# Attention products of whole units: two half-unit passes become one, in a new order of a step pair

## The chip, the cores and the metric

The kernel runs on one core of a Trainium2 chip, in one launch. The metric is the device time of that launch in microseconds (us); lower is better. It is given as the median of several runs. One further execution was recorded by the hardware profiler, and all rows quoted here come from such an execution. Names of engines in the rows: PE is the matmul engine (TensorE), PEld its weight loads, DVE VectorE, ACT ScalarE, POOL GpSimd, SP the engine that issues most of the DMAs.

## The reference

Four layers over an input of 2048 rows and 640 columns in float32, each added to its input after a layer norm: windowed attention, Fourier mixing, attention, Fourier mixing.

```python
def _A_ref(x, wqkv, wo):                  # H = 32 heads, Dh = 20, W = 8, dil = 2
    q, k, v = (x @ wqkv) split in three, (B, H, S, Dh)
    idx = pos[:, None] - (jnp.arange(W) * dil)[None, :]
    mask = idx >= 0
    kg, vg = k[:, :, idx], v[:, :, idx]   # (B, H, S, W, Dh), idx clipped at 0
    logits = jnp.einsum("bhsd,bhswd->bhsw", q, kg) * Dh ** -0.5
    attn = softmax(jnp.where(mask, logits, -1e9))
    o = jnp.einsum("bhsw,bhswd->bhsd", attn, vg)
    return o.transpose(0, 2, 1, 3).reshape(B, S, D) @ wo

def _B_ref(x, Ws_re, Ws_im, Wd_re, Wd_im):
    a, b = x @ Wd_re.T, x @ Wd_im.T
    return Ws_re @ a - Ws_im @ b

x = x + _A_ref(_layernorm(x), ...)
x = x + _B_ref(_layernorm(x), ...)
x = x + _A_ref(_layernorm(x), ...)
x = x + _B_ref(_layernorm(x), ...)
```

Each row attends to itself and the seven rows at distances 2, 4, ... 14 before it, so q·k and attn·v are eight products of 20 elements for each row and head.

## The kernel before

Every large product runs on PE in three passes over operands split in a rounded high part and a remainder (a "hi" copy on ACT, a "lo" subtraction on DVE or POOL). [...]

**Tiling of attention.** The 2048 rows are four chunks c of 512 (even rows, then odd rows); a partition holds four rows of a chunk. The 32 heads are eight groups e of four (80 columns). A unit u is one chunk and one group, u = 8c + e, 32 units in a layer. A unit's window tile holds 11 consecutive rows of k (or v) for each partition, and a strided view gives each of its four rows its eight. The units of the last chunk (24 to 31, `PAIRED`) are formed differently: two rows of a partition and two groups of heads, with one window tile for each group.

**What a unit does**, in two halves (jp) of two rows each until now. The product q·k (L423, DVE, 128 partitions by 2·8·80 = 1280 elements, q from PSUM, k from the window), then POOL adds elements 10 to 19 of each head to elements 0 to 9 (L425, 640 elements), then DVE sums the ten (L431) into the logits lg. After both halves the softmax runs once over the unit's 128 logits a partition: mask (L446, in chunks 0 and 2 only), max (L448), subtraction (L450), exp on ACT (L439), sum (L452), reciprocal (L454), weights pp (L456). Then again in halves the product of weights and v (L461, DVE, 1280 elements), and a tree of three adds over the eight window rows on POOL (L476 with 640 elements, L477 with 320, L478 with 160), the last of which writes the output tile (zo0 to zo3). Unit 31's second half has its tree on DVE.

**Buffers.** The products go through a ring of four tiles pr0 to pr3 of two rows each. The windows have a ring of five tiles (`NWIN`), loaded by SP (L409) in the order of use. q comes by a DMA (L393) to one tile qs, and ACT copies it to PSUM (L396, `q_copy`) before the unit's products. One PSUM tile, pq, holds q, the weights pp, the max, the sum and the mask side by side. Waits between engines are made for a whole tile.

**Order.** All engines run in program order, and the order in attention is written out by hand: a plan maps (step, phase) to functions, and a loop goes through steps −7 to 66 and, in each, through the names in `PHASES`. Two steps are one unit's pitch. Before, unit u has its half products at steps 2u and 2u+1 (phase qk), the reduces one step later (red1, red0), mask, max, subtraction and exp at 2u+2, sum, reciprocal and pp at 2u+3, the half av products and trees at 2u+3 (av1) and 2u+4 (av0), and its q copy at 2u−1.

**Around it in the same steps.** On PE: the qkv projections of later chunks (L354, from step −7 on), transposes of normed x and of the attention output (L319, L327), the output projection (L501), and from step 49 on the first matmuls of the next Fourier layer (L916, `z_mm`) in thirds, their number a step given by `ZTHIRDS`. On DVE in phase misc: the residual adds (L151), splits of the output weights (L555) and of Fourier matrices (L901), the lo part of the next layer's normed input (L866, on POOL or DVE). On ACT: evacuations of qkv (L361), hi and lo parts of transposes (L323, L342), row statistics. `TA` is the step of the transposes of the last chunk's rows j = 2, 3 (first three column blocks); the last two blocks and the rest of the output projection follow the loop. The Fourier layers share `T(...)`, the allocator of tiles by tag, and hold some of their weights in the tiles pr0 to pr3.

Of the kernel before, what the change touches and what calls it, by code (L numbers as in the profile page):

```python
# [20 lines left out]
D = 640  # L21
H = 32
DH = 20
# [25 lines left out]
)  # L49
TA = 65  # L50
NWARM = 18
# [20 lines left out]
def tile_layers(ctx: ExitStack, tc: tile.TileContext, x, wqkv, wo, cs, wre, wim, out):  # L72
# [161 lines left out]
    def layer_a(li, stats, handoff, prev):  # L234
# [6 lines left out]
        xnT = {}  # L241
        pcnt = [0]
        mt = {}
# [14 lines left out]

        def prod():
            pcnt[0] += 1  # L260
            return T([P, 2, W, FE], f"pr{pcnt[0] % 4}")

# [136 lines left out]
        def w_load(u, t, i=None):  # L399
            c = u // NE  # L400
            e, jp = half(u, i or 0)
            r0 = (c % 2) * 512
            if i is not None:
                r0 += 2 * jp
            n = SLOTS if i is None else SLOTS - 2
            b = kvb[e // 2][c // 2][e % 2, t, r0 : r0 + n, :]
            src = bass.AP(tensor=b.tensor, offset=b.offset, ap=[[NJ * FE, P], [1, n * FE]])
            w = wtile([P, SLOTS * FE])
            nc.sync.dma_start(w[:, : n * FE], src)  # L409
            if i is None:  # L410
                for x in range(2):
                    win[(u, x, t)] = (w, 2 * x * FE)
            else:
                win[(u, i, t)] = (w, 0)

        def wview(u, i, t, tail):
            w, off = win.pop((u, i, t))
            return bass.AP(tensor=w.tensor, offset=w.offset + off, ap=[w.ap[0], [FE, 2], [FE, W]] + tail)

        def qk_mul(u, jp):  # L420
            pr = prod()
            q = qs[u][:, 2 * jp : 2 * jp + 2].unsqueeze(2).to_broadcast([P, 2, W, FE])
            nc.vector.tensor_tensor(pr, q, wview(u, jp, 0, [[1, FE]]), op=ALU.mult)  # L423
            pv = pr.rearrange("p j w (h d) -> p (j w h) d", d=DH)
            nc.gpsimd.tensor_tensor(pv[:, :, 0:10], pv[:, :, 0:10], pv[:, :, 10:20], op=ALU.add)  # L425
            prq[(u, jp)] = pv

        def qk_red(u, jp):
            if jp == 0:
                lgs[u] = T([P, NJ, W, HE], "lg", bufs=2)  # L430
            nc.vector.tensor_reduce(  # L431
                lgs[u][:, 2 * jp : 2 * jp + 2].rearrange("p j w h -> p (j w h)"),
                prq.pop((u, jp))[:, :, 0:10],
                axis=AX.X,
                op=ALU.add,
            )
# [21 lines left out]

        def av_mul(u, jp):
            pr = prod()  # L460
            nc.vector.tensor_tensor(  # L461
                pr.rearrange("p j w (h d) -> p j w h d", d=DH),
                lgs[u][:, 2 * jp : 2 * jp + 2].unsqueeze(4).to_broadcast([P, 2, W, HE, DH]),
                wview(u, jp, 1, [[DH, HE], [1, DH]]),
                op=ALU.mult,
            )
            avq[(u, jp)] = pr

        def av_tree(u, i):
            c = u // NE  # L470
            e, jp = half(u, i)
            if e == 0:
                oo[(c, jp)] = T([P, 2, D], f"zo{(2 * c + jp) % 4}")
            pr = avq.pop((u, i))
            g = nc.vector if (u, i) == (NG - 1, 1) else nc.gpsimd
            g.tensor_tensor(pr[:, :, 0:4], pr[:, :, 0:4], pr[:, :, 4:8], op=ALU.add)  # L476
            g.tensor_tensor(pr[:, :, 0:2], pr[:, :, 0:2], pr[:, :, 2:4], op=ALU.add)  # L477
            g.tensor_tensor(oo[(c, jp)][:, :, e * FE : (e + 1) * FE], pr[:, :, 0], pr[:, :, 1], op=ALU.add)  # L478

# [123 lines left out]
        def prologue_first():  # L603
            wq_begin(0)
            for j, (k0, k1) in enumerate(((0, 3), (3, 5))):
                x_load(0, j, f"pr{j}")
                for k in range(k0, k1):
                    wq[(0, k)] = wq_load1(0, k)
            for j in range(2, NJ):
                x_load(0, j, f"pr{j}")  # L610
            for q in (1, 2, 3):
# [144 lines left out]
        for c, w, xtags in (  # L756
# [19 lines left out]
        for ph in ("peT0", "hi", "peL", "actL"):  # L776
            plan.pop((67, ph))
        at(66, "pe3w", wo_mm, c, 2, ("aux0", "aux1"), 0, 2, 0, 3)
        for i in range(2):
            at(65, "dmas", *((handoff.cw_load, 0) if first else (handoff.c_get,)), 14 + i)  # L780
        at(65, "dmar", r_load, c, 2, "xr")
        at(66, "dmar", r_load, c, 3, "xa")
        if prev is not None:
            for j2 in range(2):
                at(j2 - 3, "pe3", prev.ymm, NT - 1, j2, 0, KD)
                at(j2 - 2, "actl", prev.yout, NT - 1, j2, stats)
        last = 66
        thirds = [t for t, n in ZTHIRDS[ly].items() for _ in range(n)]
# [14 lines left out]
        else:  # L803
            at(63, "dmac", handoff.c_get, 13)

        PHASES = (
            "peT0 dma evac hi pe peL pe2 fin red0 dma2 qk sA sB av0 sD red1 sE sC exp evacA actL evacO actl sF av1 qc"
            " dmaw dmas misc dmac dmar pe3w pe3"
        ).split()
        with tc.manual_schedule(engines=ENGINES):  # L810
# [7 lines left out]
            pc_pe(67)  # L818
            pc_hi(67)
            pc_lo(67, True)  # L820
            wo_mm(c, 2, None, 0, 2, 3)
# [22 lines left out]
    class LayerB:  # L844
# [79 lines left out]
        def load_w(self):  # L924
            self.wr = T([P, 2, KD, D], "r2a", F32R)
            self.wi = []
            for k in range(KD):
# [3 lines left out]
                if k < 4:  # L931
                    wt = T([P, 2, D], f"pr{k}", F32R)
                    hl = (wt[:, 0], wt[:, 1])
# [383 lines left out]
```

## Time and profile before

| | |
|---|---|
| median of 3 runs | 1813.44 us (1812.18 to 1818.15) |
| the profiled execution, its own time | 1810.4 us |
| its span in the profile | 1808.5 us |
| mean granted PE clock | 0.992 |
| layer 0, attention | about 0 to 400 us of the span |
| layer 2, attention | about 940 to 1290 us |

A row of the view by line reads: line of the kernel, engine, operation, output tile <- input tiles with their shapes, count; then the total busy us and the mean ns of one; then the engine's idle time just before these instructions and what ended it. A row of the timeline has start, length, engine, line and operation. In the slices each digit is the busy share of a fortieth of the span (45 us) in tenths, and the chain is the work that ended last, followed back from the last instruction.

### The profile page before, as it was taken

The numbers are of one execution on the slowest core, as the hardware profiler recorded it, in microseconds if no ns is written. First come the engines' busy times: TensorE is split into PE (matmuls) and PEld (weight loads), VectorE is DVE, ScalarE is ACT, GpSimd is POOL, SyncE is SP. The second block draws the span as 40 slices with busy tenths as digits, with TensorE's granted clock in tenths as the row PEclk, the third lists the DMA queues.
The fourth block names the chain that finished last, engine by engine and source line by source line (L and its number), as shares of the span: only waits on it lengthen the run. The fifth ranks groups of instructions, "written<-read, shape, count | busy, mean of one in ns | idle before, by whom it ended". The sixth has DMA issues, their size and how long they took to land.

```text
span 1808.5 us, 26471 instructions
## 1 busy us (share of the span) xinstructions
PE 1746.1 (97%) x8798; PEld 1508.9 (83%) x8798; DVE 1380.1 (76%) x2129; ACT 818.9 (45%) x1708; POOL 640.6 (35%) x597
## 2 busy tenths in 40 slices
PE   9999997989999999999999999999899999999999
PEld 6879886777887887888888889877788888888888
DVE  5899899888768767767739988887777677676673
ACT  5544544544445445445533334444434443443441
POOL 3799898960000000000008987899400000000000
PEclk9999998999999999999999999999999999999999
DMA  6776667647789689677647856687687766876761
GB/s 233 224 263 208 208 203 247 218 164 280 273 267 332 223 270 336 221 258 229 215 132 226 278 181 199 200 296 261 218 295 257 259 226 225 265 231 223 259 210 52
DMA packets 273738, 423.59 MB, mean 234 GB/s; under 512 B 22688, under 2 KB 152736, under 8 KB 273344
## 3 DMA queue, kind: packets, MB, share of 16 engines
q1 hardware_dynamic: 270400, 419.92, 70.0%
q10 hardware_dynamic: 3200, 1.97, 0.4%
q8 instruction: 70, 1.15, 0.2%
q14 instruction: 68, 0.56, 0.1%
HBM read 336.66 MB, written 85.14 MB: 233 GB/s over the span
## 4 chain that ended last, share of the span: by engine, by line
PE 65%; DVE 12%; DMA 10%; POOL 6%; ACT 3%; issue 3%; SPq 1%; DVEq 0%; ACTq 0%; POOLq 0%
PE m L354 17%; PE aux L994 13%; PE t L1083 9%; PE m L1083 9%; PE xt L1083 4%; PE pq L1083 4%; PE aux L501 4%; DMA win<-cs_in 2%; DVE pr L423 2%; DVE pr L461 2%; PE m L916 2%; PE t L916 2%; POOL pr L476 2%; DMA c0b<-r 2%; DVE r L1077 1%
## 5 line engine op out<-in xcount | busy, mean ns | idle before, releaser
L354 PE MATMUL m<-r,s 128*128 128x480 f32 x1920 | 439.9, 384 | 5.7 <-ACT s L224 2.4
L354 PEld LDWEIGHTS m<-r,s 128*128 128x128 f32 x1920 | 357.5, 189 | 61.5 <-ACT s L224 3.8
L166 POOL TENSOR_TENSOR stats<-stats,mhalf 128x1 f32<-128x1 f32 (+1 forms) x40 | 30.4, 761 | 564.9 <-ACT stats L162 564.8
L1076 ACT CAST r<-win 128x512 fp32r<-128x512 f32 x244 | 149.4, 620 | 178.4 <-DVE win L1112 75.5
L994 PE MATMUL aux<-r2a,zo 128*128 128x320 f32 x768 | 226.5, 310 | 0.0
L476 POOL TENSOR_TENSOR pr<-pr 128x640 f32<-128x640 f32 x126 | 200.9, 1595 | 40.7 <-DVE pr L461 39.7
L423 DVE TENSOR_TENSOR pr<-pq,win 128x1280 f32<-128x1280 f32 x128 | 189.8, 1483 | 29.9 <-ACT pq L396 29.3
L994 PE MATMUL aux<-pr,zo 128*128 128x320 f32 x704 | 208.2, 308 | 0.0
L1077 DVE TENSOR_TENSOR r<-win,r 128x512 fp32r<-128x512 f32 x244 | 164.5, 686 | 46.8 <-ACT r L1076 40.7
L461 DVE TENSOR_TENSOR pr<-pq,win 128x1280 f32<-128x1280 f32 x128 | 190.8, 1491 | 4.5 <-DVE pq L456 0.2
L425 POOL TENSOR_TENSOR pr<-pr 128x640 f32<-128x640 f32 x128 | 183.4, 1433 | 18.7 <-DVE pr L423 15.6
L1083 PE MATMUL m<-r,r 128*128 128x512 f32 x600 | 154.7, 392 | 0.4 <-DVE r L1077 0.4
L994 PEld LDWEIGHTS aux<-r2a,zo 128*128 128x128 f32 x768 | 144.1, 188 | 2.0
L1083 PE MATMUL t<-r,r 128*128 128x512 f32 x498 | 135.4, 393 | 2.5 <-issue 2.5
L916 PE MATMUL m<-s,r 128*128 128x512 f32 x384 | 119.8, 399 | 15.3 <-DMA s<-c0b 6.7
L1083 PEld LDWEIGHTS m<-r,r 128*128 128x128 f32 x600 | 112.4, 188 | 25.8 <-DVE r L1077 0.7
L994 PEld LDWEIGHTS aux<-pr,zo 128*128 128x128 f32 x704 | 132.1, 188 | 2.0
L916 PE MATMUL t<-s,r 128*128 128x512 f32 x384 | 118.4, 395 | 2.3 <-DVE ot L976 1.5
L361 ACT COPY stg<-m 128x480 f32<-128x480 f32 x128 | 70.9, 556 | 104.6 <-PE m L354 94.0
L477 POOL TENSOR_TENSOR pr<-pr 128x320 f32<-128x320 f32 x126 | 114.4, 908 | 9.9
L431 DVE TENSOR_REDUCE lg<-pr 128x64 f32<-128x640 f32 x128 | 103.9, 811 | 17.7 <-POOL pr L425 17.4
L1083 PEld LDWEIGHTS t<-r,r 128*128 128x128 f32 x498 | 93.4, 188 | 24.6 <-issue 3.3
(269 smaller groups left out, 3246.3 us busy)
## 6 DMA issues: line engine op xcount, KB each, us to landing
win<-cs_in SPq DMA_DIRECT2D x358, 256.0 KB, 4.1
r<-xc SPq DMA_DIRECT2D x240, 256.0 KB, 4.3
win<-kvb SPq DMA_DIRECT2D x96, 440.0 KB, 4.8
xa<-cs_in SPq DMA_DIRECT2D x124, 256.0 KB, 4.2
win<-kvb SPq DMA_DIRECT2D x64, 360.0 KB, 5.3
xc<-stg SPq DMA_DIRECT2D x40, 512.0 KB, 3.1
kvb<-stg SPq DMA_DIRECT2D x60, 320.0 KB, 3.9
xr<-xs SPq DMA_DIRECT2D x40, 320.0 KB, 3.2
```

The source lines that it names most:

```text
L354: nc.tensor.matmul(mt[g][:, : 3 * F], st[:, a, k], wq[q][:, b, k], start=n == 0, stop=n == 14)
L423: nc.vector.tensor_tensor(pr, q, wview(u, jp, 0, [[1, FE]]), op=ALU.mult)
L425: nc.gpsimd.tensor_tensor(pv[:, :, 0:10], pv[:, :, 0:10], pv[:, :, 10:20], op=ALU.add)
L431: nc.vector.tensor_reduce(lgs[u][:, 2 * jp : 2 * jp + 2].rearrange("p j w h -> p (j w h)"), prq.pop((u, jp))[:, :, 0:10], axis=AX.X, op=AL ...
L461: nc.vector.tensor_tensor(pr.rearrange("p j w (h d) -> p j w h d", d=DH), lgs[u][:, 2 * jp : 2 * jp + 2].unsqueeze(4).to_broadcast([P, 2, ...
L476: g.tensor_tensor(pr[:, :, 0:4], pr[:, :, 0:4], pr[:, :, 4:8], op=ALU.add)
L477: g.tensor_tensor(pr[:, :, 0:2], pr[:, :, 0:2], pr[:, :, 2:4], op=ALU.add)
L916: self.last = nc.tensor.matmul(self.z[t][k], self.xn[c][:, a, j, k * P : (k + 1) * P], self.ct[s][:, b], start=s == 0 and i == 0, stop=s = ...
L994: self.last = nc.tensor.matmul(self.ym[e][:, :320], zt[(k, a, ri)][:, j2 * P : (j2 + 1) * P], w[:, e * 320 : (e + 1) * 320], start=(k, a, ...
L1076: nc.scalar.copy(hi, raw)
L1077: nc.vector.tensor_tensor(lo, raw, hi.bitcast(F32), op=ALU.subtract)
L1083: nc.tensor.matmul(bank, w(a, kb), hl[b], start=start and (a, b) == (0, 0), stop=stop and (a, b) == (1, 0),)
```

## The change

Products, POOL adds, logit reduces and the first two tree steps are issued once for a unit, over four rows of a partition:

- the ring of four product tiles becomes one tile of four rows for q·k (prA) and one for av (prB); the Fourier layers and the first loads of x use parts of the same two tiles;
- `qk_mul` is one product of 2560 elements and one POOL add of 1280; `qk_red` one reduce of 1280 elements into 128 logits; `av_mul` one product of 2560; `av_tree` has steps of 1280 and 640 elements and then two adds of 160, one for each pair of rows. In the paired units each product remains two instructions of 1280, since they read two window tiles. Unit 31's tree is split in halves between POOL and DVE;
- the order in a step pair: at the even step 2u qk of u, then sum, reciprocal and pp of u−1; at the odd step av of u−1, the reduce of u, mask, max and subtraction of u on DVE, then on ACT the q copy of u+1 and the exp of u. av and tree of a unit are at step 2u+3 as a whole;
- both window loads of a paired unit are issued at 2u−2 (k) and 2u+1 (v), before at 2u−2 and 2u−1, 2u+1 and 2u+2;
- the loop ends one step earlier (65): `TA` goes from 65 to 64, and with it the last output projection, row loads and the last loads of Fourier matrices; `ZTHIRDS` is unchanged, so in layer 2 four thirds and in layer 0 one third of step 64 now stand behind these transposes on PE.

The counts of instructions go from 2067 to 1907 on DVE and from 599 to 411 on POOL; ACT, PE and SP have as many as before.

```diff
-TA = 65
+TA = 64
...
-        def prod():
-            pcnt[0] += 1
-            return T([P, 2, W, FE], f"pr{pcnt[0] % 4}")
+        def prod(tag):
+            return T([P, NJ, W, FE], tag)
...
-        def qk_mul(u, jp):
-            pr = prod()
-            q = qs[u][:, 2 * jp : 2 * jp + 2].unsqueeze(2).to_broadcast([P, 2, W, FE])
-            nc.vector.tensor_tensor(pr, q, wview(u, jp, 0, [[1, FE]]), op=ALU.mult)
+        def wviews(u, t, tail):
+            paired = u in PAIRED
+            for i in range(1 + paired):
+                w = win.pop((u, i if paired else None, t))
+                js = slice(2 * i, 2 * i + 2) if paired else slice(0, NJ)
+                yield js, bass.AP(tensor=w.tensor, offset=w.offset, ap=[w.ap[0], [FE, js.stop - js.start], [FE, W]] + tail)
+
+        def qk_mul(u):
+            pr = prod("prA")
+            for js, w in wviews(u, 0, [[1, FE]]):
+                q = qs[u][:, js].unsqueeze(2).to_broadcast([P, js.stop - js.start, W, FE])
+                nc.vector.tensor_tensor(pr[:, js], q, w, op=ALU.mult)
             pv = pr.rearrange("p j w (h d) -> p (j w h) d", d=DH)
             nc.gpsimd.tensor_tensor(pv[:, :, 0:10], pv[:, :, 0:10], pv[:, :, 10:20], op=ALU.add)
...
+        def av_mul(u):
+            pr = prod("prB")
+            for js, w in wviews(u, 1, [[DH, HE], [1, DH]]):
+                nc.vector.tensor_tensor(
+                    pr[:, js].rearrange("p j w (h d) -> p j w h d", d=DH),
+                    lgs[u][:, js].unsqueeze(4).to_broadcast([P, js.stop - js.start, W, HE, DH]),
+                    w,
+                    op=ALU.mult,
+                )
...
-            pr = avq.pop((u, i))
-            g = nc.vector if (u, i) == (NG - 1, 1) else nc.gpsimd
-            g.tensor_tensor(pr[:, :, 0:4], pr[:, :, 0:4], pr[:, :, 4:8], op=ALU.add)
-            g.tensor_tensor(pr[:, :, 0:2], pr[:, :, 0:2], pr[:, :, 2:4], op=ALU.add)
-            g.tensor_tensor(oo[(c, jp)][:, :, e * FE : (e + 1) * FE], pr[:, :, 0], pr[:, :, 1], op=ALU.add)
+            pr = avq.pop(u)
+            for js in (slice(0, 2), slice(2, 4)) if u == NG - 1 else (slice(0, NJ),):
+                g = nc.vector if js.start else nc.gpsimd
+                g.tensor_tensor(pr[:, js, 0:4], pr[:, js, 0:4], pr[:, js, 4:8], op=ALU.add)
+                g.tensor_tensor(pr[:, js, 0:2], pr[:, js, 0:2], pr[:, js, 2:4], op=ALU.add)
+                for i in range(js.start // 2, js.stop // 2):
+                    e, jp = half(u, i)
+                    v = pr[:, 2 * i : 2 * i + 2]
+                    g.tensor_tensor(oo[(c, jp)][:, :, e * FE : (e + 1) * FE], v[:, :, 0], v[:, :, 1], op=ALU.add)
...
             if u in PAIRED:
                 for i in range(2):
-                    at(2 * u + i - 2, "dmaw", w_load, u, 0, i)
-                    at(2 * u + i + 1, "dmaw", w_load, u, 1, i)
+                    at(2 * u - 2, "dmaw", w_load, u, 0, i)
+                    at(2 * u + 1, "dmaw", w_load, u, 1, i)
...
-            for jp in range(2):
-                s = 2 * u + jp
-                at(s, "qk", qk_mul, u, jp)
-                at(s + 1, "red0" if jp else "red1", qk_red, u, jp)
-                at(s + 3, "av0" if jp else "av1", av_mul, u, jp)
-                at(s + 3, "av0" if jp else "av1", av_tree, u, jp)
+            at(2 * u, "qk", qk_mul, u)
+            at(2 * u + 1, "red", qk_red, u)
             for i, ph in enumerate(("sA", "sB", "sC")):
-                at(2 * u + 2, ph, soft, u, i)
-                at(2 * u + 3, ("sD", "sE", "sF")[i], soft, u, 3 + i)
-            at(2 * u + 2, "exp", soft_exp, u)
+                at(2 * u + 1, ph, soft, u, i)
+                at(2 * u + 2, ("sD", "sE", "sF")[i], soft, u, 3 + i)
+            at(2 * u + 1, "exp", soft_exp, u)
+            at(2 * u + 3, "av", av_mul, u)
+            at(2 * u + 3, "av", av_tree, u)
...
-                    tp(60 if j < 2 else 67, "o", c, j, 3, 5, "aux0" if j < 2 else "pq", 256 * (j % 2))
+                    tp(60 if j < 2 else 66, "o", c, j, 3, 5, "aux0" if j < 2 else "pq", 256 * (j % 2))
...
-        last = 66
+        last = 65
...
         PHASES = (
-            "peT0 dma evac hi pe peL pe2 fin red0 dma2 qk sA sB av0 sD red1 sE sC exp evacA actL evacO actl sF av1 qc"
+            "peT0 dma evac hi pe peL pe2 fin dma2 qk sD sE sF av red sA sB sC evacA actL evacO actl qc exp"
             " dmaw dmas misc dmac dmar pe3w pe3"
         ).split()
```

More of the change, by code (lines that the diff above doesn't have):

```diff
@@ L409, in w_load, with qk_red @@
             nc.sync.dma_start(w[:, : n * FE], src)
[L410 to L418, printed above, removed]
-        def qk_mul(u, jp):
-            pr = prod()
-            q = qs[u][:, 2 * jp : 2 * jp + 2].unsqueeze(2).to_broadcast([P, 2, W, FE])
-            nc.vector.tensor_tensor(pr, q, wview(u, jp, 0, [[1, FE]]), op=ALU.mult)
+            win[(u, i, t)] = w
+        def wviews(u, t, tail):
[9 more added lines that the diff above has]
+                nc.vector.tensor_tensor(pr[:, js], q, w, op=ALU.mult)
             pv = pr.rearrange("p j w (h d) -> p (j w h) d", d=DH)
             nc.gpsimd.tensor_tensor(pv[:, :, 0:10], pv[:, :, 0:10], pv[:, :, 10:20], op=ALU.add)
[L426 to L430, printed above, removed]
+            prq[u] = pv
+        def qk_red(u):
+            lgs[u] = T([P, NJ, W, HE], "lg", bufs=2)
             nc.vector.tensor_reduce(
[L432 to L435, printed above, removed]
+                lgs[u].rearrange("p j w h -> p (j w h)"), prq.pop(u)[:, :, 0:10], axis=AX.X, op=ALU.add
             )
@@ L457, in soft, with av_tree @@
                 lgs[u] = pp
[L459 to L469, printed above, removed]
[L470 to L478 removed]
+        def av_mul(u):
[7 more added lines that the diff above has]
+                )
+            avq[u] = pr
+        def av_tree(u):
+            c = u // NE
+            for i in range(2):
+                e, jp = half(u, i)
+                if e == 0:
+                    oo[(c, jp)] = T([P, 2, D], f"zo{(2 * c + jp) % 4}")
+            pr = avq.pop(u)
[4 more added lines that the diff above has]
+                for i in range(js.start // 2, js.stop // 2):
+                    e, jp = half(u, i)
+                    v = pr[:, 2 * i : 2 * i + 2]
+                    g.tensor_tensor(oo[(c, jp)][:, :, e * FE : (e + 1) * FE], v[:, :, 0], v[:, :, 1], op=ALU.add)
         def r_load(c, j, tag="xr"):
@@ L604, in prologue_first, with x_first @@
             wq_begin(0)
+            x0 = T([P, NJ, D], "prA")
+            def x_first(j):
+                xnT[(0, j)] = x0[:, j]
+                nc.sync.dma_start(x0[:, j], xin[0][:, j, :])
             for j, (k0, k1) in enumerate(((0, 3), (3, 5))):
-                x_load(0, j, f"pr{j}")
+                x_first(j)
                 for k in range(k0, k1):
@@ L931, in load_w @@
                 if k < 4:
-                    wt = T([P, 2, D], f"pr{k}", F32R)
+                    if k % 2 == 0:
+                        pair = T([P, 2, 2, D], ("prA", "prB")[k // 2], F32R)
+                    wt = pair[:, k % 2]
                     hl = (wt[:, 0], wt[:, 1])
```

19 lines of the change are left out of this document (9 added, 10 removed).

## The prediction

> **What bounds the kernel now.** I read the page's busy shares, the slices and the chain first, then the windows of the two attention layers (the stretches in which POOL works), because only they are edited. The columns of the window rows are the busy time of PE, PEld, DVE, ACT and POOL, the granted clock, the DMA share and GB/s.
>
> ```profile
> PE 1746.1 (97%) x8798; PEld 1508.9 (83%) x8798; DVE 1380.1 (76%) x2129; ACT 818.9 (45%) x1708; POOL 640.6 (35%) x597
> POOL 3799898960000000000008987899400000000000
> ...
> PE 65%; DVE 12%; DMA 10%; POOL 6%; ACT 3%; issue 3%; SPq 1%; DVEq 0%; ACTq 0%; POOLq 0%
> ```
> ```profile
> 0.00:400.00 400.00, 370.45 (x1866) 319.28 (x1867) 343.34 (x494) 201.29 (x494) 329.64 (x311) 0.97 0.67 218
> 940.00:1290.00 350.00, 334.56 (x1722) 293.18 (x1721) 301.39 (x432) 144.47 (x354) 302.58 (x277) 0.99 0.72 234
> ```
> ```profile
> 80.00:120.00 40.00, 34.36 (x152) 28.17 (x152) 39.11 (x49) 18.08 (x43) 34.32 (x30) 0.96 0.80 266
> 120.00:160.00 40.00, 40.00 (x210) 35.47 (x209) 37.39 (x50) 21.29 (x55) 38.33 (x39) 1.00 0.66 209
> 280.00:320.00 40.00, 29.60 (x141) 25.31 (x141) 36.66 (x52) 15.53 (x41) 35.13 (x33) 0.83 0.70 226
> 1040.00:1160.00 120.00, 120.00 (x637) 107.77 (x636) 101.69 (x147) 50.80 (x128) 99.34 (x92) 1.00 0.62 198
> 1200.00:1240.00 40.00, 36.70 (x199) 32.26 (x197) 33.43 (x55) 20.47 (x52) 37.18 (x37) 0.96 0.91 318
> 1240.00:1280.00 40.00, 33.59 (x168) 27.88 (x168) 32.57 (x49) 13.44 (x35) 38.43 (x36) 1.00 0.69 232
> ```
>
> Three things are to be seen. PE is idle for only 29.6 + 15.4 = 45 us in the 750 us of attention, so no saving there can exceed 45 us unless PE work itself shrinks, and this change leaves PE's work alone. DVE is idle for 105 us and POOL for 118 us in the same 750 us, so each has slack on average. But the slack is uneven: from 80 to 120 DVE is the full engine (39.11 of 40), from 120 to 160 and from 1040 to 1160 PE is, and from 1200 to 1280 POOL is (37.18 and 38.43). A longer DVE pair costs time in the first kind of stretch, nothing in the second; a shorter POOL costs or gains in the third.
>
> One unit on DVE in a dense stretch (start, length, instruction), and its q copy on ACT:
>
> ```profile
> 157.18 1.48 DVE L423 TENSOR_TENSOR pr<-pq,win 128x1280 f32<-128x1280 f32 x1
> ...
> 160.72 0.48 DVE L151 SCALAR_TENSOR_TENSOR xr<-aux,xr 128x320 f32<-128x320 f32 x1
> ...
> 161.13 1.49 DVE L423 TENSOR_TENSOR pr<-pq,win 128x1280 f32<-128x1280 f32 x1
> 162.72 0.40 DVE L452 TENSOR_REDUCE pq<-lg 128x16 f32<-128x128 f32 x1
> ...
> 164.38 1.49 DVE L461 TENSOR_TENSOR pr<-pq,win 128x1280 f32<-128x1280 f32 x1
> 165.78 0.81 DVE L431 TENSOR_REDUCE lg<-pr 128x64 f32<-128x640 f32 x1
> 166.51 1.48 DVE L423 TENSOR_TENSOR pr<-pq,win 128x1280 f32<-128x1280 f32 x1
> ```
> ```profile
> 165.90 0.43 ACT L396 COPY pq<-qs 128x320 f32<-128x320 f32 x1 [1.25 <-DVE pr L461]
> ```
>
> The unit takes 166.51 − 157.18 = 9.33 us, of which 0.41 (160.72 to 161.13) is a residual add that not every unit has: 8.92 without it. An instruction that needs nothing of the one before starts while that one still runs (the reduce at 165.78, 1.40 after the product at 164.38, which lasts 1.49); one that needs its predecessor starts 0.03 to 0.1 after its end. The q copy runs behind the second av product while DVE does the reduce, so the next product finds q ready at 166.51.
>
> **The change part by part.** The durations (busy time, mean ns of one, idle before):
>
> ```profile
> L476 POOL TENSOR_TENSOR pr<-pr 128x640 f32<-128x640 f32 x126 | 200.9, 1595 | 40.7 <-DVE pr L461 39.7
> L461 DVE TENSOR_TENSOR pr<-pq,win 128x1280 f32<-128x1280 f32 x128 | 190.8, 1491 | 4.5 <-DVE pq L456 0.2
> L425 POOL TENSOR_TENSOR pr<-pr 128x640 f32<-128x640 f32 x128 | 183.4, 1433 | 18.7 <-DVE pr L423 15.6 <-PE m L354 2.4
> L477 POOL TENSOR_TENSOR pr<-pr 128x320 f32<-128x320 f32 x126 | 114.4, 908 | 9.9
> L431 DVE TENSOR_REDUCE lg<-pr 128x64 f32<-128x640 f32 x128 | 103.9, 811 | 17.7 <-POOL pr L425 17.4
> L478 POOL TENSOR_TENSOR zo<-pr 128x160 f32<-128x160 f32 x126 | 68.6, 544 | 9.9
> L448 DVE TENSOR_REDUCE pq<-lg 128x16 f32<-128x128 f32 x64 | 25.0, 391 | 2.2
> L456 DVE TENSOR_TENSOR pq<-lg,pq 128x128 f32<-128x128 f32 x64 | 18.9, 296 | 2.2
> L450 DVE TENSOR_TENSOR lg<-lg,pq 128x128 f32<-128x128 f32 x64 | 17.7, 277 | 0.1
> L454 DVE RECIPROCAL pq<-pq 128x16 f32<-128x16 f32 x64 | 16.4, 256 | 0.1
> ```
>
> *POOL.* Before, a unit has 2 × (1.433 + 1.595 + 0.908 + 0.544) = 8.96 us. From 320 to 640 elements the tree step grows by 0.687, or 2.15 ns an element, which leaves about 0.2 us that does not grow. So the merged add comes to about 2.65, the merged steps to 2.97 and 1.60, the last two stay at 0.544 each: 8.3 us, 0.64 less a unit, 41 us over 64 units. It is worth time only where POOL sets the pace, which are the seven units of 1200 to 1280 and, as I estimate, two elsewhere: at most 9 × 0.64 = 6 us. I take −4, since in the same units PE waits for other things too.
>
> *DVE, a unit.* The merged product costs 1.40 + 1.49 = 2.89 to its end, where a second instruction merely followed it at 1.40; merging saves only the overlap's counterpart, under 0.1. The new order has, one after the other: qk 2.8 + 0.1, sum 0.42, reciprocal 0.29, pp 0.33, av 2.75, reduce 1.52, max 0.42, subtraction 0.28. In the old order the long products of another half stood between these; now each of them but qk needs the instruction before it. Behind the subtraction comes the q copy of the next unit on ACT (it writes the tile pq, which the subtraction reads) and then the next qk, which needs it: 0.05 + 0.43 + 0.03 = 0.51 in which DVE has nothing, unless a residual add or another odd job stands there. The sum is 9.4 against 8.92, +0.5 a unit (a unit with the mask +0.6). If nothing absorbed it: 64 × 0.5 = 32, about a quarter of it under residual adds, so +25. That is the upper bound; the lower is 0, if PE's lead covers it. Where DVE is the full engine (80 to 120: about four units) I take 4 × 0.5 less a covered one, +1.5. In the stretches with PE holes (280 to 320, 1200 to 1280, some 20 units) DVE has 3.3 of 40 us idle, about 0.9 a unit, more than the 0.5, so most is absorbed: +3 of 10. Elsewhere PE is full and DVE has its slack: 0.
>
> [...]
>
> *ACT.* The exp moves from the even step to the place right behind the q copy, with its input ready. It waited for long before, in ACT's order, ahead of evacuations:
>
> ```profile
> ACT lg L439 <- DVE lg L450: 145.9, 52, 7.0
> SPq L409 <- DVE pr L423: 26.3, 18, 3.6
> ```
>
> Now the q copy waits for the subtraction instead, and the evacuation of the next step stands behind both. ACT is busy 45% of the time; I cost this at 0, between −3 (evacuations freed from the old wait) and +3 (evacuations late, then PE's banks).
>
> *DMA and SP.* The count is the same. In the eight paired units of each layer both half windows are issued together, the second a step earlier, into the same five buffers; what SP has behind such a load waits while it waits for a buffer (18 times, 26.3 us). A window is still free after its own product. 0, between −2 and +3.
>
> *DVE beside a longer POOL instruction.* Two forms of one line, with the same shape and other operands, and a doubled one:
>
> ```profile
> L901 DVE TENSOR_TENSOR s<-win,s 128x512 fp32r<-128x512 f32 x34 | 23.3, 684 | 4.0 <-ACT s L888 4.0
> L901 DVE TENSOR_TENSOR s<-stg,s 128x512 fp32r<-128x512 f32 x14 | 15.5, 1118 | 0.0
> L555 DVE TENSOR_TENSOR r2a<-zo,r2a 128x640 fp32r<-128x640 f32 x4 | 6.1, 1513 | 0.0
> L127 DVE TENSOR_TENSOR r2a<-xa,r2a 128x640 fp32r<-128x640 f32 x10 | 8.2, 818 | 3.0 <-ACT r2a L123 3.0
> ```
>
> The 14 of the attention layers last 0.43 longer than the 34 of the same shape, and the four splits of the output weights 0.70 longer than ten equal splits elsewhere; POOL is busy beside the slow ones. The products, with one operand in PSUM, do not show it. If the excess is a wait for the POOL instruction in flight, instructions twice as long double it: 14 × 0.43 + 4 × 0.70 = 8.9 us more of DVE, 0 if it is not that. These stand where PE waits for DVE; I take a third, +3. [...]
>
> *The end of layer 2.* PE's last order:
>
> ```profile
> 1278.19 0.62 PE L916 MATMUL m<-s,r 128*128 128x512 f32 x2
> ...
> 1282.82 0.82 PE L319 MATMUL aux<-ident,zo 128*128 128x128 f32 x6
> 1283.88 0.82 PE L327 MATMUL aux<-zo,nident 128*128 128x384 f32 x2 [0.24 <-ACT zo L323]
> 1284.89 2.90 PE L501 MATMUL aux<-r2a,zo 128*128 128x320 f32 x18 [0.19 <-ACT zo L342]
> ```
>
> The four thirds of the Fourier matmuls from 1278.19 to 1282.82 (4.6 us) covered the time until unit 30's tree was done. With the transposes a step earlier they stand in front of these thirds and wait for the now whole tree of unit 30 (2.97 + 1.60 + 0.54 behind the av product), while the thirds come after: up to 4.6 lost, 2 if they then hide the evacuation and unit 31's tree. +3; in layer 0, with one third behind, +0.5.
>
> **Sum:** 1.5 + 3 − 4 + 3 + 3.5 = +7 on the profiled run. That run took 1810.4 us (span 1808.5), 3.0 below the median of 1813.44; 1817.4 there is 1820 as a median.
>
> **The rivals.** *DVE's pair binds nearly everywhere* (no lead of PE absorbs it, since every later PE input hangs on DVE): +25, so 1838. For it: 39.11 of 40. Against: PE full over 1040 to 1160 with 18 us of DVE idle there. *Nothing measurable:* the +0.5 sits inside PE's full stretches, the POOL relief and the tail cancel: 1814. For it: 97% PE. *Faster:* POOL's 0.64 and the 0.08 of each merge come through, the windows and product tiles come free sooner, and PE's holes close by a quarter: 45 / 4 ≈ −12, so 1801. It decides if the holes are POOL's and if residual adds or other DVE jobs stand in the q copy's gap. For it: 38.43 of 40 for POOL while PE has 6.4 us idle. Against: the holes at 280 to 320 come with DVE at 36.66. [...]
>
> **How the numbers follow.** About 0.3% (5.4 us) is what a measurement of this kernel can tell from no change: 1808 to 1819. Forecast 0.35 (1815 to 1826, a tenth of it within the bound); DVE binds 0.15; nothing 0.25; faster 0.25 (a little of it within the bound). That gives slower 0.46, the same 0.31, faster 0.23. The range of 1803 to 1838 takes in the no-change case and most of the outer two, with the ±3 of ACT and SP.
>
> **What would show it.** Right: idle before the qk product released by the q copy in most units, about 0.5 each, without an add there; dense units of 9.4; POOL instructions of about 2.65 and 2.97; L901 on stg well above 1118; PE idle at the transposes near the end of layer 2. Wrong: PE's idle in attention under 40 us (then faster), or above 60 (then DVE binds); merged products much under 2.8; POOL instructions that grow by less or more than 2.15 ns an element, which would move the relief by tens of us.

## The result, and the profile after

The changed kernel takes 1824.39 us (median of 9 runs, 1820.86 to 1830.28) against 1813.79 us (9 runs of the kernel before, 1812.18 to 1818.15). The ratio is 1.0058 with a 95% interval of 1.0043 to 1.0073: slower by about 10.6 us, clear of noise, though small.

The page of the changed kernel, busy time by engine, the slices of POOL and the chain by engine:

```profile
PE 1757.7 (96%) x8798; PEld 1515.0 (83%) x8798; DVE 1391.0 (76%) x1969; ACT 820.8 (45%) x1708; POOL 603.9 (33%) x409
POOL 3778887860000000000007887889400000000000
...
PE 56%; DVE 16%; DMA 9%; ACT 4%; issue 4%; POOL 3%; SPq 0%; DVEq 0%; ACTq 0%; POOLq 0%
```

POOL's busy time falls by 36.7 us, as intended, and buys nothing: the chain gives 4 points to DVE and takes 9 from PE. The windows of the changed kernel (columns as before: PE, PEld, DVE, ACT, POOL, clock, DMA share, GB/s), and, last, the row of the kernel before for the stretch that turned out to matter:

```profile
80.00:120.00 40.00, 33.74 (x138) 28.08 (x137) 38.59 (x34) 15.29 (x35) 27.18 (x17) 0.87 0.80 259
1000.00:1040.00 40.00, 34.81 (x156) 28.83 (x154) 36.34 (x38) 11.62 (x27) 33.32 (x21) 0.96 0.81 257
1240.00:1280.00 40.00, 36.33 (x195) 31.50 (x193) 33.57 (x46) 17.88 (x43) 39.36 (x28) 0.99 0.79 270
```
```profile
1000.00:1040.00 40.00, 40.00 (x188) 34.61 (x188) 38.59 (x52) 15.11 (x35) 38.01 (x36) 0.96 0.82 266
```

From 1000 to 1040 PE goes from full to 34.81 us, while DVE, which sets the pace, has also become less busy: it stands idle inside its own units.

To find the place of the loss I counted PE's matmuls line by line. PE runs the same matmuls in both kernels, so the start of the same matmul, compared with the first profile of the kernel before, says how far a kernel is behind at that point, and differences between such points say where it fell behind (the order of the matmuls on PE changes only around 385 and from 1278 to 1284). The columns are stretches of the former kernel's span in us; each number is what was lost there, worked out from the starts in the traces:

| profile | 67–131 | 131–204 | 204–350 | 350–940 | 940–979 | 979–1040 | 1040–1194 | 1194–1249 | 1249–1382 | to the end |
|---|---|---|---|---|---|---|---|---|---|---|
| before, again | 0.0 | 0.1 | −0.1 | 1.8 | 0.0 | −0.6 | −0.1 | −1.0 | 1.8 | 0.3 |
| after | 3.7 | 0.8 | 4.4 | 1.6 | 0.9 | 7.8 | 0.8 | −3.0 | 2.7 | 0.0 |
| after, again | 3.7 | 0.8 | −0.6 | 2.5 | 0.8 | 7.7 | 2.0 | −2.5 | 5.6 | −1.1 |

What both profiles of the changed kernel show is 3.7 us around units 3 to 6 of layer 0, 7.7 or 7.8 us at units 3 to 9 of layer 2, and 2.5 to 3 us gained from 1194 to 1249, where POOL sets the pace. Stretches in which profiles of one kernel differ by several us (204 to 940, 1249 to 1382) prove nothing. The columns add up to 20 us, more than the medians, because the former kernel's profiled run (1810.4) was shorter than any of its nine timed runs and the changed kernel's (1830.28) the longest of its nine. The clock granted to PE does not explain the two losses: in the second profile of the changed kernel it stood at 0.50 for 3.4 us in each of these two stretches, just as in the kernel before, and the losses are the same.

The groups (busy us, mean ns of one, idle before) that answer to those before:

```profile
L423 POOL TENSOR_TENSOR prA<-prA 128x1280 f32<-128x1280 f32 x64 | 171.0, 2672 | 23.3 <-DVE prA L421 22.2
L473 POOL TENSOR_TENSOR prB<-prB 128x1280 f32<-128x1280 f32 x62 | 183.2, 2954 | 88.8 <-DVE prB L456 88.8
L474 POOL TENSOR_TENSOR prB<-prB 128x640 f32<-128x640 f32 x62 | 99.7, 1609 | 4.9
L421 DVE TENSOR_TENSOR prA<-pq,win 128x2560 f32<-128x2560 f32 x48 | 135.6, 2824 | 39.4 <-ACT pq L394 38.4
L905 DVE TENSOR_TENSOR s<-stg,s 128x512 fp32r<-128x512 f32 x14 | 22.5, 1619 | 0.4 <-ACT s L892 0.4
L555 DVE TENSOR_TENSOR r2a<-zo,r2a 128x640 fp32r<-128x640 f32 x4 | 7.4, 1852 | 0.0
```

The waits of the q·k products for the q copy (us in all, times, longest), first in the kernel before, then in the changed one, whole and half products together:

```profile
DVE pr L423 <- ACT pq L396: 29.3, 17, 4.9
```
```profile
DVE prA L421 <- ACT pq L394: 42.6, 40, 4.7
```

The 17 waits have become 40. The splits beside POOL have grown: L905 on stg from 1118 to 1619 ns, L555 from 1513 to 1852, 7.0 and 1.4 us in sum, although neither was edited. In the second profile of the changed kernel the four are as long (1843 ns), while the 14 are at 1437, 4.5 us more than before. A fifth split of the output weights, on the tile ot, goes from 1408 to 2712 ns in the first profile and to 2748 in the second.

The dense unit of layer 2 on DVE, with the q copy on ACT and what PE does after it (start, length, instruction, idle before and releaser):

```profile
1028.62 1.48 DVE L428 TENSOR_REDUCE lg<-prA 128x128 f32<-128x1280 f32 x1
...
1030.87 0.29 DVE L444 TENSOR_TENSOR lg<-lg,pq 128x128 f32<-128x128 f32 x1
1031.70 2.83 DVE L421 TENSOR_TENSOR prA<-pq,win 128x2560 f32<-128x2560 f32 x1 [0.54 <-ACT pq L394]
...
1035.74 2.83 DVE L456 TENSOR_TENSOR prB<-pq,win 128x2560 f32<-128x2560 f32 x1
1038.48 1.48 DVE L428 TENSOR_REDUCE lg<-prA 128x128 f32<-128x1280 f32 x1
...
1040.41 0.29 DVE L444 TENSOR_TENSOR lg<-lg,pq 128x128 f32<-128x128 f32 x1
```
```profile
1031.24 0.43 ACT L394 COPY pq<-qs 128x320 f32<-128x320 f32 x1 [4.56 <-DVE lg L444]
...
1040.77 0.43 ACT L394 COPY pq<-qs 128x320 f32<-128x320 f32 x1 [6.80 <-DVE lg L444]
...
1041.79 0.59 ACT L321 CAST s<-xt 128x512 fp32r<-128x512 f32 x1
```
```profile
1042.43 0.50 PE L325 MATMUL xt<-s,nident 128*128 128x512 f32 x1 [2.72 <-ACT s L321]
```

The unit (with mask) takes 1038.48 − 1028.62 = 9.86 us, and 0.54 of it is DVE waiting for the q copy. In the former kernel such a unit took 9.09, from the starts of two successive max reduces:

```profile
1006.52 0.39 DVE L448 TENSOR_REDUCE pq<-lg 128x16 f32<-128x128 f32 x1
...
1015.61 0.39 DVE L448 TENSOR_REDUCE pq<-lg 128x16 f32<-128x128 f32 x1
```

How it reaches PE is in the ACT rows: ACT runs in order, the q copy waits 6.80 us for the subtraction at 1040.41, and the hi copy of a transpose stands behind it; PE, at the remainder of that transpose, waits 2.72. Such waits of PE for a hi copy, over the whole span, in the kernel before, in the changed one, and in the one with the q copy behind av and POOL in halves (below):

```profile
PE xt L327 <- ACT s L323: 4.7, 2, 2.6
```
```profile
PE xt L325 <- ACT s L321: 12.6, 7, 3.6
```
```profile
PE xt L325 <- ACT s L321: 3.6, 2, 2.7
```

### The profile page after: what moved, and what is told of

It is laid out like the page before. It is cut to its first block, busy times and chain, and to the rows that moved or that the text cites. A ratio compares the mean times of both kernels' runs of the same rounds, so it can differ in the third digit from the quotient of the medians.

```text
span 1828.5 us, 26113 instructions
## 1 busy us (share of the span) xinstructions
PE 1757.7 (96%) x8798; PEld 1515.0 (83%) x8798; DVE 1391.0 (76%) x1969; ACT 820.8 (45%) x1708; POOL 603.9 (33%) x409
## 4 chain that ended last, share of the span: by engine, by line
PE 56%; DVE 16%; DMA 9%; ACT 4%; issue 4%; POOL 3%; SPq 0%; DVEq 0%; ACTq 0%; POOLq 0%
PE aux L1000 13%; PE t L1089 10%; PE m L1089 9%; PE m L352 8%; PE xt L1089 5%; PE pq L1089 5%; PE aux L501 4%; DVE prA L421 3%; DVE prB L456 3%; DMA win<-cs_in 2%; DMA xc<-stg 2%; DVE lg L428 1%; POOL prB L473 1%; DVE s L905 1%; DMA c0b<-r 1%
## 5 line engine op out<-in xcount | busy, mean ns | idle before, releaser
L473 POOL TENSOR_TENSOR prB<-prB 128x1280 f32<-128x1280 f32 x64 | 186.3, 2911 | 91.0 <-DVE prB L456 91.0
L421 DVE TENSOR_TENSOR prA<-pq,win 128x2560 f32<-128x2560 f32 (+1 forms) x80 | 181.7, 2288 | 45.0 <-ACT pq L394 42.6
L456 DVE TENSOR_TENSOR prB<-pq,win 128x2560 f32<-128x2560 f32 (+1 forms) x80 | 181.6, 2286 | 5.5 <-POOL zo L478 2.8
L423 POOL TENSOR_TENSOR prA<-prA 128x1280 f32<-128x1280 f32 x64 | 171.0, 2672 | 23.3 <-DVE prA L421 22.2
L1000 PE MATMUL aux<-prA,zo 128*128 128x320 f32 x384 | 114.1, 307 | 0.0
L1082 ACT CAST s<-win 128x512 fp32r<-128x512 f32 x116 | 71.5, 621 | 81.3 <-DVE win L1118 31.5
L1118 DVE TENSOR_TENSOR win<-win,win 128x512 f32<-128x512 f32 x111 | 76.4, 690 | 39.4 <-DMA win<-cs_in 38.1
L474 POOL TENSOR_TENSOR prB<-prB 128x640 f32<-128x640 f32 x64 | 102.4, 1601 | 5.0
```

The lines of the kernel that those rows point to most:

```text
L421: nc.vector.tensor_tensor(pr[:, js], q, w, op=ALU.mult)
L456: nc.vector.tensor_tensor(pr[:, js].rearrange("p j w (h d) -> p j w h d", d=DH), lgs[u][:, js].unsqueeze(4).to_broadcast([P, js.stop - js. ...
L473: g.tensor_tensor(pr[:, js, 0:4], pr[:, js, 0:4], pr[:, js, 4:8], op=ALU.add)
L474: g.tensor_tensor(pr[:, js, 0:2], pr[:, js, 0:2], pr[:, js, 2:4], op=ALU.add)
L1000: self.last = nc.tensor.matmul(self.ym[e][:, :320], zt[(k, a, ri)][:, j2 * P : (j2 + 1) * P], w[:, e * 320 : (e + 1) * 320], start=(k, a, ...
L1082: nc.scalar.copy(hi, raw)
```

## The experiments

All ratios are to the kernel before, measured beside it; the intervals are 95%.

| kernel | median us | ratio | interval |
|---|---|---|---|
| before, again | 1815.04 | 0.9996 | 0.9982 to 1.0009 |
| after, again | 1828.55 | 1.0065 | 1.0049 to 1.0080 |
| q copy behind av, evacuations ahead | 1830.92 | 1.0081 | 1.0065 to 1.0098 |
| last transposes a step later | 1828.75 | 1.0068 | 1.0055 to 1.0081 |
| POOL in halves | 1823.82 | 1.0046 | 1.0034 to 1.0058 |
| q copy behind av, evacuations ahead, POOL in halves | 1826.55 | 1.0057 | 1.0042 to 1.0072 |
| q copy behind av | 1823.93 | 1.0046 | 1.0033 to 1.0059 |
| q copy behind av, POOL in halves | 1816.41 | 1.0004 | 0.9994 to 1.0014 |
| q copy behind av, POOL in halves in layer 0 | 1816.92 | 1.0001 | 0.9990 to 1.0013 |
| q copy behind av, POOL and DVE in halves | 1819.97 | 1.0020 | 1.0008 to 1.0031 |

And what each lost in the stretches that tell something, from the traces as above:

| profile | 67–131 | 979–1040 | 1194–1249 |
|---|---|---|---|
| after, again | 3.7 | 7.7 | −2.5 |
| q copy behind av, evacuations ahead | 4.3 | 4.2 | −1.1 |
| last transposes a step later | 3.6 | 9.3 | −2.4 |
| POOL in halves | 0.3 | 6.2 | −0.8 |
| both of these (evacuations ahead) | −0.6 | 4.0 | −2.4 |
| q copy behind av | 6.0 | 2.1 | −1.3 |
| q copy behind av, POOL in halves | −0.2 | 1.9 | −0.4 |
| the same, halves in layer 0 only | −0.4 | 2.4 | −0.7 |
| q copy behind av, all in halves | 1.9 | 4.8 | −1.4 |

**The changed kernel again** (no edit).

> The changed kernel itself once more, as the measure for the other three on one chip. Every theory: 1.0058 of the kernel before, with its interval of 1.0043 to 1.0073, and dense units of 9.5 us without the mask and 9.9 with it, as in its first profile. If its units or their sum differ by some us from that profile, that is what two profiles of one kernel differ by.

1.0065, its interval overlapping the first. The two stable losses are there again, 3.7 and 7.7; the 4.4 at the end of layer 0 is not (−0.6).

**The kernel before again** (no edit).

> The kernel before once more, profiled a second time, for what two profiles and two sets of runs of one kernel differ by. Every theory: ratio 1.000, dense units as in its first profile (8.9 to 9.2 us). If its first attention layer ends several us later or earlier than in the first profile, differences of that size at the end of that layer say nothing.

0.9996; its second profile is 2.2 us behind the first at the end, picked up outside the edited stretches.

**The q copy behind av, evacuations ahead of it.**

```diff
-"... qk sD sE sF av red sA sB sC evacA actL evacO actl qc exp"
+"... qk sD sE sF evacA actL evacO actl av qc red sA sB sC exp"
```

> The q copy is issued after av instead of after the subtraction, so it can run while DVE reduces; ACT's evacuations stay in front of it. Theory 1 (the round trip from the subtraction over ACT to the next product sets the longer unit): dense units fall by about 0.5, from 9.9 to 9.4 with the mask and from 9.5 to 9.0 without, idle before the product L421 for the q copy goes to near 0, and of the 9 us that layer 2 loses between 960 and 1040 some 4 to 5 return, some 2 in layer 0: ratio 1.002 to 1.003. Rival (the chain of dependent small instructions or the POOL waits set the unit): units stay within 0.1 of 9.9 and 9.5, ratio 1.005 to 1.006.

The units did what the theory said: 9.31 with the mask, 8.98 without, and the loss at the start of layer 2 fell from 7.7 to 4.2. In units 3 to 6 of layer 0 nothing changed (4.3), so that loss has another cause. But the whole got no better (1.0081, outside the ranges of theory and rival). The waits of DVE for ACT show a price of the evacuations' new place:

```profile
DVE lg L440 <- ACT pq L394: 25.4, 10, 5.1
DVE pq L442 <- ACT pq L394: 23.0, 12, 5.5
```

The mask add and the max (they write the tile pq's max, or read its mask) now wait 48 us in all for a q copy that stands behind evacuations waiting for PE (121.3 us of such waits in this run). This run alone decided neither for nor against the round trip; the next ones do.

**POOL in halves.**

```diff
-            nc.gpsimd.tensor_tensor(pv[:, :, 0:10], pv[:, :, 0:10], pv[:, :, 10:20], op=ALU.add)
+            pq4 = pr.rearrange("p j w (h d) -> p j (w h) d", d=DH)
+            for x in range(2):
+                ph = pq4[:, 2 * x : 2 * x + 2].rearrange("p j g d -> p (j g) d")
+                nc.gpsimd.tensor_tensor(ph[:, :, 0:10], ph[:, :, 0:10], ph[:, :, 10:20], op=ALU.add)
...
-            for js in (slice(0, 2), slice(2, 4)) if u == NG - 1 else (slice(0, NJ),):
-                g = nc.vector if js.start else nc.gpsimd
+            for js in (slice(0, 2), slice(2, 4)):
+                g = nc.vector if u == NG - 1 and js.start else nc.gpsimd
```

> POOL's adds and tree steps are issued in halves again, DVE's stay whole. Theory 3 (DVE instructions with two SBUF inputs wait out longer POOL instructions): the 14 of L905 on stg return from 1619 to about 1120 ns, the 4 of L555 from 1852 to about 1510, 8 us of DVE; if these stand on the path, 2 to 5 us less than the changed kernel, ratio 1.003 to 1.005. Rival (POOL's 0.64 us a unit is worth more than the waiting): POOL busy up by some 35 us and 2 to 5 us more than the changed kernel, ratio 1.007 to 1.009.

1.0046. The loss at units 3 to 6 is gone (0.3 instead of 3.7). The groups of this kernel:

```profile
L908 DVE TENSOR_TENSOR s<-stg,s 128x512 fp32r<-128x512 f32 x14 | 17.3, 1249 | 1.4 <-ACT s L895 1.4
L558 DVE TENSOR_TENSOR r2a<-zo,r2a 128x640 fp32r<-128x640 f32 x4 | 4.7, 1168 | 0.0
```

These are L905 and L555 of the changed kernel: 1619 (1437 in its second profile) to 1249 ns and 1852 to 1168; the theory had 1120 and 1510. All five splits of the output weights, which stand in units 3 to 6, take 10.1 us in both profiles of the changed kernel and 6.8 here: 3.4 less, as much as the stretch regains. In the start of layer 2, which has none of these splits, the loss stays (6.2). In the median the gain is 4.7 us, but the intervals of the two kernels overlap; with the q copy moved (below) they do not.

**The last transposes a step later.**

```diff
-TA = 64
+TA = 65
```

> The transposes of the last chunk go back to step 65, behind the thirds of step 64. Theory 2 (the thirds behind the transposes cost time at the end of layer 2): 2 to 4.6 us less than the changed kernel, ratio about 1.004. Rival (thirds and waits only change places): within 1 us of the changed kernel, or slower by up to 2 us, since the output projection now waits for the evacuation of these transposes.

1828.75 beside 1828.55: no gain. The theory's 2 to 4.6 us are not there, although the spread of the few runs leaves room for about 2; the rival's "within 1 us" fits.

**Both: q copy behind av with evacuations ahead, POOL in halves.**

> The q copy behind av with the evacuations ahead of it, and POOL's work in halves. Theory (longer POOL instructions cost units 3 to 6 of layer 0 some 4 us, the round trip costs the first ten units of layer 2 some 4 us): both gains add up, layer 0 as before up to its 480th projection matmul, layer 2's first third behind by 2 to 4 us, ratio 1.002 to 1.004. Rival (moving the evacuations ahead costs what the q copy gains): ratio 1.005 to 1.007, with DVE's mask and max waiting for the q copy.

1.0057, the rival's figure. Units 3 to 6 are as before the change (−0.6), and the start of layer 2 loses 4.0, so both gains are there where they were expected, and are lost elsewhere; DVE's mask and max wait for the q copy as in the first of these kernels (rows below).

**The q copy behind av, evacuations left where they were.**

```diff
-"... qk sD sE sF av red sA sB sC evacA actL evacO actl qc exp"
+"... qk sD sE sF av qc red sA sB sC evacA actL evacO actl exp"
```

> The q copy behind av, with ACT's evacuations of the odd step left behind it, in their place after the subtraction. Theory (in the run with the evacuations ahead, the q copy waited for evacuations that wait for PE, and that ate its gain): DVE's mask and max no longer wait for the q copy, ratio 1.003 to 1.005. Rival (the evacuations, now behind the q copy and av, come late and PE waits for its banks): PE idle with the evacuation L359 as releaser grows to over 5 us, ratio 1.006 to 1.009.

1.0046, at the theory's end. Its reason held by half: DVE's mask and max still wait for the q copy, but 23 us in all (12.7 and 10.3) instead of 48. The start of layer 2 loses 2.1 instead of 7.7. Its interval still touches that of the changed kernel, so this run alone is not proof for the whole time; with POOL in halves it is:

**The same, with POOL in halves.**

> As the run with the q copy right behind av, with POOL's work in halves as well. Theory: 3 to 4 us less than that run, ratio 1.001 to 1.003, since POOL's length and the round trip are paid in different units. Rival (what remains is the dependent chain and POOL's order): no better than POOL's halves alone, 1.004 to 1.005.

1.0004 (0.9994 to 1.0014), 7.5 us less than without POOL's halves, where the theory had 3 to 4: no longer to be told from the kernel before, and apart from each of the two edits alone (1.0033 to 1.0059, 1.0034 to 1.0058). The unit in layer 2 is now

```profile
1015.29 1.48 DVE L431 TENSOR_REDUCE lg<-prA 128x128 f32<-128x1280 f32 x1
...
1017.62 0.29 DVE L447 TENSOR_TENSOR lg<-lg,pq 128x128 f32<-128x128 f32 x1
1017.83 2.82 DVE L421 TENSOR_TENSOR prA<-pq,win 128x2560 f32<-128x2560 f32 x1
...
1024.60 1.48 DVE L431 TENSOR_REDUCE lg<-prA 128x128 f32<-128x1280 f32 x1
```

9.31 us, the product starting 0.21 behind the subtraction's start and before its end, with no wait. The waits of DVE for the q copy, first in this kernel, then in the one with the evacuations ahead:

```profile
DVE lg L443 <- ACT pq L394: 12.1, 8, 2.3
...
DVE pq L445 <- ACT pq L394: 10.3, 7, 3.4
```
```profile
DVE lg L443 <- ACT pq L394: 26.9, 11, 5.2
...
DVE pq L445 <- ACT pq L394: 23.3, 13, 6.2
```

The two differ only in the place of the evacuations, and by 10 us in the median.

**The same, with halves in layer 0 only.**

> The q copy right behind av; POOL's work in halves in layer 0 and whole in layer 2. Theory (long POOL instructions hurt where DVE has instructions with two SBUF inputs, the splits of weights that only layer 0 has; elsewhere POOL's 0.64 us a unit is a gain): layer 0 as in the run with halves everywhere, and in layer 2 the seven POOL-paced units gain the 2 to 3 us that the changed kernel gained there: ratio 0.998 to 1.000. Rival (halves are worth as much in layer 2): 1 to 3 us more than the run with halves everywhere, ratio 1.001 to 1.002.

1.0001 (0.9990 to 1.0013), undecided between the two: POOL whole in layer 2 neither gains nor loses more than the nearly 3 us that the two intervals leave. Against the kernel with POOL whole everywhere, 1823.93, it is 7.0 us faster (the two were measured beside different runs of the kernel before), so within this error the price of POOL's long instructions is paid in layer 0, the layer with the splits.

**The same order, with POOL and DVE in halves.**

```diff
-            for i in range(1 + paired):
+            for i in range(2):
...
+            for x in range(2):
+                nc.vector.tensor_reduce(lf[:, n * x : n * x + n], pv[:, n * x : n * x + n, 0:10], axis=AX.X, op=ALU.add)
```

> The q copy right behind av, and DVE's products and reduces in halves too, as POOL's work: only the new order of the pair is left of the change. Theory by the trace (a merged instruction saves DVE under 0.1): units of DVE longer by 0 to 0.2, time within 2 us of the run with POOL's halves, ratio 1.000 to 1.002. [...]

```profile
1010.35 2.88 DVE L422 TENSOR_TENSOR prA<-pq,win 128x1280 f32<-128x1280 f32 x2
...
1019.85 2.88 DVE L422 TENSOR_TENSOR prA<-pq,win 128x1280 f32<-128x1280 f32 x2
```

The unit takes 9.50, 0.19 more than with DVE's instructions whole, for three merges: 0.06 each. That is within the theory's 0 to 0.2. The medians differ by 3.6 us (by 3.1 from the kernel with halves in layer 0 only, which ran beside the same runs of the kernel before), more than the theory's 2, with intervals that overlap. The start of layer 2 loses 4.8 instead of 1.9; ten units longer by 0.19 come to 1.9 of this 2.9, and the rest is not explained.

None of these beats the kernel before; two equal it.

## Why the prediction was right or wrong

The sign was right, and the size too small: +7 us was forecast, 10.6 measured. By its own terms it was less right than that. Two terms were too small, and two did not come; that these last two, −4 and +3.5, cancel in the sum is luck.

- **The longer unit (+1.5 in layer 0, +3 at PE's holes, 0 elsewhere).** The mechanism is shown: a stall of 0.54 for the q copy in each dense unit (forecast 0.51), gone when the copy is issued behind av. The units came out longer than the forecast 9.4, and 9.5 with the mask: 9.54 and 9.86. The place was wrong. "Elsewhere PE is full and DVE has its slack: 0" failed between 979 and 1040: 7.7 us were lost there. The row of the former kernel that would have told it is the one from 1000 to 1040 above: PE at 40.00 and DVE at 38.59, both full. Five units with the mask were longer by 0.6 to 0.8 us there and the three behind them, without it, by 0.4 to 0.5; DVE fell behind by 4.9 us in these eight, and PE by 7.7 with the waits for hi copies that stand behind the q copy and the exp on ACT. How much is the unit's length and how much ACT's queue, no run separates. The +3 at PE's holes stays open: from 204 to 350 the two profiles of the changed kernel give 4.4 and −0.6. In layer 0, where the 1.5 was put, DVE's waits for the q copy were mostly covered by the splits standing at the end of the odd step, as the working allowed for, and moving the copy won nothing (4.3 and 6.0 lost with the copy moved, 3.7 without).
- **DVE beside longer POOL instructions (+3 of at most 8.9).** Mechanism right, share too small. With the fifth split, which the working left out, DVE's excess grew by 9.7 us in the first profile and 7.1 in the second, against the bound of 8.9, and the runs put the price in time at 4.7 (POOL in halves alone, 1828.55 to 1823.82) to 7.5 us (with the q copy moved, 1823.93 to 1816.41). Of this, 3.4 us are traced to the five splits in units 3 to 6; the other 14 stand between 285 and 390, where two profiles of one kernel differ too much to tell their share. One place shows the wait instruction by instruction; DVE's rows and POOL's of the changed kernel:

```profile
79.61 2.39 DVE L555 TENSOR_TENSOR r2a<-zo,r2a 128x640 fp32r<-128x640 f32 x1
...
87.11 1.28 DVE L555 TENSOR_TENSOR r2a<-zo,r2a 128x640 fp32r<-128x640 f32 x1
```
```profile
78.65 2.67 POOL L423 TENSOR_TENSOR prA<-prA 128x1280 f32<-128x1280 f32 x1
84.81 2.89 POOL L473 TENSOR_TENSOR prB<-prB 128x1280 f32<-128x1280 f32 x1 [3.50 <-DVE prB L456]
87.78 2.01 POOL L474 TENSOR_TENSOR prB<-prB 128x640 f32<-128x640 f32 x1
```

  POOL's add ends at 81.32 and the split at 82.00, 0.68 later; POOL's tree step ends at 87.70 and the next split at 88.39, 0.69 later. Both splits started while POOL was in flight and finished a fixed time after it: they waited it out. So did all five in both profiles of the changed kernel (0.68 to 0.69), and twelve of the 14 shorter ones in each (0.54 to 0.55). The wait for the POOL instruction in flight, an "if" in the working, is what these rows show, and the sum should have taken more of its 8.9.
- **POOL's relief (−4).** POOL's instructions came out as worked out (2.672, 2.954 and 1.609 against 2.65, 2.97 and 1.60), and its time fell by 36.7 us. From 1194 to 1249 the kernel did gain 2.5 to 3 us, in both profiles, but that this is POOL's relief is not shown: in the table above a kernel with POOL in halves gains 2.4 there, and the two with POOL whole in layer 2 and the q copy right behind av gain 1.3 and 0.7. Of the gain about 1 us was given back by 1300. PE lost 5.2 at one place, where it waited for residual adds that stand at the end of DVE's step, behind a reduce that waits for POOL; the last row is the same group of matmuls in the kernel before:

```profile
1277.72 1.49 DVE L428 TENSOR_REDUCE lg<-prA 128x128 f32<-128x1280 f32 x1 [1.24 <-POOL prA L423]
...
1279.87 0.48 DVE L151 SCALAR_TENSOR_TENSOR xa<-aux,xa 128x320 f32<-128x320 f32 x1
```
```profile
1280.41 7.28 PE L501 MATMUL aux<-r2a,s 128*128 128x320 f32 x30 [3.10 <-DVE xa L151]
```
```profile
1263.03 4.66 PE L501 MATMUL aux<-r2a,s 128*128 128x320 f32 x30 [0.51 <-DVE xa L151]
```

  PE pays twice: 2.6 us more of waiting, and then 2.6 more for the same 30 matmuls, because the clock granted to it was 0.50 from 1279.4 to 1286.2: the matmuls start 0.27 apart until then and 0.15 apart after it. It regains 4.5 around this place, where the kernel before waited 2.14 for a lo part and 2.33 for a DMA.

  With POOL whole or in halves in layer 2 the medians were alike (1816.92 and 1816.41), so of the 4 us nothing was seen.
- **The end of layer 2 (+3) and of layer 0 (+0.5).** Wrong: moving the transposes back won nothing. The transposes did wait for unit 30's tree, but 0.97 us, because PE came to them only at 1295.55, when the tree was nearly through, and the thirds behind them then filled the time in which ACT makes the hi and lo parts:

```profile
1296.90 0.66 PE L317 MATMUL aux<-ident,zo 128*128 128x128 f32 x4 [0.97 <-POOL zo L478]
1297.80 0.82 PE L325 MATMUL aux<-zo,nident 128*128 128x384 f32 x2 [0.24 <-ACT zo L321]
```

  The working set a full wait against the old times of PE, while the new order also delayed PE.
- **The rivals.** DVE's pair did not bind everywhere (between 1040 and 1194 only 0.8 to 2.0 were lost). "Faster" was built on POOL's relief, of which nothing was seen, and on merges being worth something on DVE; by the last run each is worth 0.06 us, which agrees with the 0.08 read from the starts (a product of 1.49 us, the next instruction 1.40 to 1.41 after its start).

What stays open: why the evacuations ahead of the q copy cost 10 us when POOL is in halves. The longer waits of DVE are shown, and that they are the whole price is not; by the starts of PE's matmuls the largest part falls between 204 and 350 (6.8 us lost against 1.1), where single profiles tell little. Of the 2 us that remain at the start of layer 2 with the copy moved, DVE's units with the mask (9.30 to 9.42 against 9.10 to 9.30) account for 0.8, and no run tried to shorten the chain of dependent small instructions further.

## What to carry to other kernels

Merging instructions on one engine lengthens each (POOL's add here from 1433 to 2672 ns), and of DVE's 19 splits with two SBUF inputs 17 waited out what POOL had in flight (they ended 0.54 to 0.69 us behind it), while the whole products, with one operand in PSUM, all took 2.81 to 2.83 us: look for such unedited instructions before making POOL's longer. When a new order puts a copy on another engine behind the last instruction of a step, its whole round trip can be exposed (here 0.54 us in each dense unit); issue it as soon as the tile's last reader is through, and look at what stands around it in the other engine's queue. And a full engine is a cover only if it is ahead: where two engines were both nearly full (40.00 and 38.59 of 40 us), a longer unit on one was paid.

## What the runs showed of the hardware that was not expected

The waiting between DVE and POOL went both ways. In the rows above, POOL's L474 at 87.78 took 2.01 us where its mean is 1.609, beside the split that had waited (87.11 to 88.39). The six L474 that started while such a split was under way took 1.87 to 2.03 us, and none of the others over 1.59. One wait of PE came with more loss than its own length: with the 3.10 us before 1280.41 came a granted clock of 0.50 for 6.8 us, and 30 matmuls took 7.28 us, where the kernel before, with 0.51 of wait, took 4.66. And the length of an unedited DVE instruction was no constant here: the same four splits took 1513 ns on average in the kernel before, 1852 in the changed one and 1168 with POOL in halves, by what POOL had in flight when they started.
